# Reading a strip transpose's source over 128 partitions and planning all moves anew, in a fused attention and Mish kernel on one core

## The chip, the cores and the metric

The kernel runs on one core of a Trainium2 chip. The time is the device time of a whole execution in microseconds; lower is better. The median of three runs of the kernel before is 477.22 us (476.9 to 479.27).

## The reference, cut to what matters

One block of a transformer with modulation by a condition, all in float32. S = 2048 rows, D = 512 columns, 32 heads of 16, F = 1792 hidden columns.

```python
mod = (silu(c) @ w_mod).reshape(1, 6, 1, -1)
sa, ca, ga, sb, cb, gb = (mod[:, i] for i in range(6))
h = layernorm(x) * (1 + ca) + sa
q, k, v = heads(h @ wqkv)                      # phi(t) = where(t > 0, t + 1, exp(t)) + 1e-6
kv, z = einsum("bhsd,bhse->bhde", phi(k), v), einsum("bhsd->bhd", phi(k))
o = einsum("bhqd,bhde->bhqe", phi(q), kv) / (einsum("bhqd,bhd->bhq", phi(q), z)[..., None] + 1e-6)
x = x + ga * (o @ wo)
h = layernorm(x) * (1 + cb) + sb
x = x + gb * (mish(h @ w1 + b1) @ w2)          # mish(t) = t * tanh(softplus(t))
```

## The kernel before, in words

The 2048 rows are four row blocks (b = 0 to 3) of 512 rows, each of four strips of 128 rows (t = 0 to 3). A product of float32 accuracy is three matmuls of rounded parts: every operand is split into an upper part (name ending in h, made by ACT, L1034) and a rest (ending in l, made by VectorE, L1040), and h·h, h·l and l·h are added up.

The first part of the program, to about 190 us, is the attention. After it comes the second layer norm of every strip (`norm_job`): sums, a small rsqrt chain rs_n partly on POOL (L348), the normalization (on ACT for b < 2, else on ACT or VectorE in turn, L359), and a store of the normalized strip to the DRAM buffer nd (L389). The FFN's first product needs the normalized block with columns on the partitions. `squares_job` therefore reads nd back in an order in which VectorE's transposes of 32x32 squares (L1530, y_n to hf_n) finish the full transpose; the reads are L1521, four per row block, and each waits for all four stores of its row block. ACT scales and shifts the four chunks hf_n (L1533). Meanwhile the strips of x + ga·o themselves (the tiles r) are completed by accumulating loads r<-in_x_dram on POOL ("joins", L1578) and stored to the output (L838), which the end of the program reads again.

The FFN works on two halves, row blocks 0 and 1 (L = 0) and 2 and 3 (L = 2), and both products are done by a scheme with seven multiplications in place of eight: `pair` multiplies for pair g of 0 to 6 (256 hidden columns) into p_a, p_s and others (L1259), with operands a and s from w1 (pieces w1p, read as two DMAs per pair in `rows_job`, L1058, sums s at L1079) and b and t from hf_n; ACT copies a partial result to u (L1274), VectorE adds c_a (L1280), ACT takes Mish to u_a (L1283), which is split into l_m for `unit`'s seven products m1 to m7 with w2 (pa to pd, L1344; their weights wt_m are DMAs from w2d and w2t).

Nothing of this order is written by hand. `drive` fixes the order in which every engine's instructions are issued, with a planner: every piece of work is a job with a due time and an earliest time, `best_job` takes for each engine the due job that can start, and `emit` moves a model clock on. DMAs may go to either queue, SP or POOL (ANY), whichever is free by the model. A load's model cost is one number, `late`:

```python
wire[0] = max(wire[0], t0 + cost + 1.4) + late
late = wire[0] + 1.3 - end
```

The due times are in the table `T`; `SHIFT` moves the due time and earliest time of single jobs by name. On the chip each engine then executes its rows strictly in this order, and each DMA queue issues in its order, so a row that waits holds those behind it.

Of the kernel before, what the change touches and what calls it, by code (L numbers as in the profile page):

```python
# [27 lines left out]
TINY = 1e-6  # L28

T = {'pre': 2,  # L30
 'pre_due': 89.2,
 'pre_at': -0.2,
 'pre_step': 12.0,
 'join_at': 90.0,
 'join_due': 106.4,
 't0_due': 5.3,
 'kept': 0,
 'early': 4,
 'slack': 3.1,
# [1 line left out]
 'store_later': 8.7,  # L41
 'row_lead': 20.6,
 'columns': 90.8,
 'column_lead': 23.7,
 'rows_early': 11.9,
 'lead_a': 4,
 'lead_l': 12,
 'lead_r': 14,
 'sum_lead': 5,
 'row_0': 31.4,  # L50
 'row_step': 12.5,
 'blocks': 14.2,
 'blocks_early': 22.0,
 'out_due': 53.4,
 'out_at': 21.3,
 'early_due': 67.9,
 'early_at': -0.5,
 'norm_due': 52.1,
# [22 lines left out]
 'r_due': 2.2,
 'out01': 58.5,
 'sum_store': 9.8,
 'half_due': 8.3,
 'sums_late': 1.5,
# [28 lines left out]
 'mish': 66.7,
 'first_at': 45.4,
 'first_due': 158.9,
 'parts_first': [-1.8, 1.4, 1.9, 4.2, 7.0, 11.0, 12.4],
 'parts_last': [-1.2, 1.4, 2.8, 4.2, 6.6, 15.7, 13.0],
 'ahead_first': 2.8,
 'ahead_last': 4.3,  # L120
 'turn_right': -0.2,
 'guard': 99.0,
 'hold': -0.1,
 'near': 3.4}

SHIFT = {'blocks_job w2r 2 0': (-0.4, -1.2),
 'blocks_job w2r 3 0': (0.0, -2.6),
 'blocks_job w2r 5 0': (4.4, 12.9),
 'load_r ANY': (12.6, 0.0),
 'norm_job x1 1 0': (-3.0, 0.0),  # L130
 'norm_job x1 1 2': (2.0, 0.0),
 'norm_job x1 2 1': (-18.3, -14.8),
 'right_job r 2 m4 5': (-4.4, 0.0),
 'right_job r 2 m6 3': (4.4, 7.5),
 'rows_job w1p 0 0 0': (-1.3, 1.0),
 'rows_job w1p 0 2 0': (-2.9, 0.0),
 'rows_job w1p 0 5 0': (-1.4, 0.0),
 'rows_job w1p 0 6 0': (5.3, -9.0),
 'split_steps ACT #44': (-23.4, 0.0),
 'split_steps ACT #8': (-6.0, 0.0),  # L140
 'step cq 0 1': (7.3, 0.0),
 'step pc 2 6': (5.3, 0.0),
 'step qr 2 2 #2': (3.3, 0.0),
 'step qr 2 3': (3.2, 0.0),
 'step qr 3 0': (3.0, 0.0),
 'step x1 0 2 #2': (16.6, -12.8),
 'steps DVE': (-16.3, 0.0),
 'stores t0 0': (27.3, 0.0),
 'sums_job w2r 1 0': (-6.7, 0.0),
 'turns DVE': (0.7, 0.0)}  # L150

@with_exitstack
def block_kernel(ctx: ExitStack, tc: tile.TileContext, x, wqkv, wo, w1, b1t, w2, c, wmodt, out):
# [229 lines left out]
    nd, yd = {}, {}  # L383
# [456 lines left out]
    hf, op_b = {}, {}  # L840
# [6 lines left out]
    PE, DVE, ACT, POOL, SP, ANY = range(6)  # L847
# [20 lines left out]
    def dma_(fn, makes=(), needs=(), queue=ANY, size=LATE):  # L868
        return step_(queue, 0.0, fn, needs, makes, size)
# [5 lines left out]
    def add_job(gen, due, at=0.0):  # L875
# [639 lines left out]
    def squares_job(b):  # L1515

        for c in range(4):
            def go(q, c=c):
                if c == 0:
                    yd["n", b] = big.tile([P, 4 * 512], F32, tag="Y", name=f"y_n_{b}", bufs=YS)  # L1520
                q.dma_start(yd["n", b][32 * c:32 * (c + 1), :].rearrange("q (m s) -> q m s", s=P),  # L1521
                            nd["n", b][c, :, :].rearrange(LANES[b], q=32))
            yield dma_(go, [("y", b)] if c == 3 else (), [("n", b, t) for t in range(4)], size=1.3 * LATE,
                       queue=(ANY, SP, POOL)[T['y_queue']] if b < 2 else ANY)
# [578 lines left out]
```

## Time and profile before

| | before |
|---|---|
| median of 3 runs | 477.22 us (476.9 to 479.27) |
| profiled execution, its own time | 478.1 us |
| its span on the core | 476.4 us |
| PE busy | 465.3 us (98%) |
| DVE (VectorE) busy | 414.9 us (87%) |
| ACT busy | 333.9 us (70%) |
| HBM traffic over the span | 222 GB/s |
| granted TensorE clock | 1.00 |

Rows of the profile give a start and a duration in us, engine, line, operation, tiles, and in brackets how long the engine stood idle just before and what ended that. "POOL" and "SPq" rows of a DMA are its issue; a DMA lands later. TensorE (PE) executes in order, so what counts is where it stands still.

### The profile page before, as it was taken

The page shows a single profiled execution, that of the slowest core. Times are in us where ns is not written, and L with a number is a line of the kernel's source. Part 1 is how long each engine was busy: PE and PEld are TensorE (multiplying, and loading weights), DVE is VectorE, ACT ScalarE, POOL GpSimd, SP SyncE. Part 2 cuts the span into 40 slices and gives each one's busy share as a digit, 9 for nine tenths or more (in the row PEclk, how much of TensorE's full clock was granted, in tenths as well). Part 3 has the DMA queues.
Part 4 walks back from the last instruction along what each step waited for, and adds up shares of the span by engine and source line. Part 5 has one row for each costly group of instructions (what it writes and reads, how often), then busy time and mean ns, then how long its engine had stood idle before and what let it go on. Part 6 is the DMA issues. An engine that isn't in the chain of part 4 may idle for free.

```text
span 476.4 us, 7262 instructions
## 1 busy us (share of the span) xinstructions
PE 465.3 (98%) x2260; PEld 381.5 (80%) x2260; DVE 414.9 (87%) x808; ACT 333.9 (70%) x614; POOL 164.7 (35%) x237
## 2 busy tenths in 40 slices
PE   8999999999999999899999999999999999999996
PEld 6788888888788888677787888888888888888886
DVE  6989989888999984698998999997796596999984
ACT  6776776849758995888987998675568555555430
POOL 4684331122220442644542222412221226426340
PEclk9999999999999999999999999999999999999999
DMA  8998699257765589998599736895531569999977
GB/s 304 400 349 228 163 194 278 74 163 225 254 154 180 161 281 275 239 268 301 171 269 345 238 118 207 165 300 154 174 113 46 154 205 225 264 292 229 191 120 134
DMA packets 83800, 102.48 MB, mean 215 GB/s; under 512 B 29481, under 2 KB 55345, under 8 KB 83506
## 3 DMA queue, kind: packets, MB, share of 16 engines
q1 hardware_dynamic: 56560, 58.48, 39.3%
q0 software_dynamic: 23888, 42.49, 37.8%
q10 hardware_dynamic: 3314, 1.05, 1.1%
q8 instruction: 18, 0.29, 0.3%
q14 instruction: 20, 0.16, 0.1%
HBM read 71.57 MB, written 34.34 MB: 222 GB/s over the span
## 4 chain that ended last, share of the span: by engine, by line
PE 76%; DMA 10%; ACT 6%; DVE 4%; issue 2%; POOL 1%; ACTq 0%; SPq 0%; DVEq 0%; POOLq 0%
PE p_a L1259 13%; PE pa L1344 11%; PE pc L1344 6%; PE p_s L1259 5%; PE pd L1344 4%; DMA out_dram<-r 4%; DMA r<-in_x_dram 3%; PE pq_a L545 3%; PE pb L1344 3%; PE gacc L212 2%; PE pk L213 2%; PE pk L212 2%; PE gacc L214 2%; PE gacc L213 2%; PE pk L214 2%
## 5 line engine op out<-in xcount | busy, mean ns | idle before, releaser
L1283 ACT ACTIVATE u_a<-c_a,b1c 128x512 f32<-128x512 f32 x42 | 30.3, 720 | 18.6 <-DVE c_a L1280 16.6
L1218 POOL DMA_DIRECT2D wt_m<-w2t x27 | 22.7, 1056 | 43.5 <-ACT l_m_3h L1034 8.8
L1409 POOL DMA_DIRECT2D out_dram<-turned x20 | 24.3, 1687 | 34.3 <-DVE turned L1397 34.3
L1274 ACT ACTIVATE u<-p_a 128x512 f32<-128x512 f32 x42 | 24.8, 591 | 15.6 <-PE p_a L1259 15.2
L1280 DVE TENSOR_TENSOR c_a<-p_s,u 128x512 f32<-128x512 f32 x28 | 19.2, 686 | 6.5 <-ACT u L1274 4.2
L1218 POOL DMA_DIRECT2D wt_m<-w2d x16 | 15.1, 1143 | 14.2 <-PE pa L1344 10.2
L1233 DVE TENSOR_TENSOR u_a<-u_a,u_a 128x512 f32<-128x512 f32 x28 | 18.5, 685 | 0.0
L348 POOL TENSOR_TENSOR rs_n<-rs_n,half 128x1 f32<-128x1 f32 x16 | 11.0, 691 | 20.6 <-DVE rs_n L1487 11.6
L1058 POOL DMA_DIRECT2D w1p<-w1d x16 | 12.4, 780 | 16.2 <-DVE a_1l L1040 6.6
L1530 DVE STREAM_TRANSPOSE hf_n<-y_n 128x512 f32<-128x512 f32 x16 | 10.4, 687 | 7.4 <-DMA y_n<-nd 7.4
L443 ACT ACTIVATE e_k<-pk 128x512 f32<-128x512 f32 x15 | 8.9, 591 | 10.2 <-PE pk L214 10.2
L1533 ACT ACTIVATE hf_n<-hf_n,mc 128x512 f32<-128x512 f32 x16 | 12.1, 805 | 3.9 <-DVE hf_n L1530 3.9
L348 POOL TENSOR_TENSOR rs_x<-rs_x,half 128x1 f32<-128x1 f32 (+1 forms) x10 | 7.8, 786 | 15.9 <-DVE rs_x L343 14.7
L446 DVE SCALAR_TENSOR_TENSOR ku<-e_k,relu_k 128x512 f32<-128x512 f32 x15 | 10.7, 715 | 2.9 <-ACT relu_k L444 2.7
L1280 DVE TENSOR_TENSOR c_a<-p_a,u 128x512 f32<-128x512 f32 x14 | 9.6, 689 | 4.0 <-PE p_a L1259 3.4
L1673 DVE SCALAR_TENSOR_TENSOR q<-e_q,relu_q 128x512 f32<-128x512 f32 x16 | 10.9, 689 | 0.6 <-ACT relu_q L1669 0.6
L1040 DVE TENSOR_TENSOR l_m_4l<-u_a,l_m_4h 128x512 fp32r<-128x512 f32 x12 | 8.2, 687 | 3.4 <-ACT l_m_4h L1034 3.4
L324 DVE SCALAR_TENSOR_TENSOR wm<-wm,sc_row 128x512 f32<-128x512 f32 x16 | 10.6, 681 | 0.0
L1795 DVE SCALAR_TENSOR_TENSOR q<-q,rd 128x512 f32<-128x512 f32 x16 | 10.6, 688 | 0.0
L1311 ACT ACTIVATE u_a<-p_a,b1c 128x512 f32<-128x512 f32 x14 | 9.5, 680 | 1.5 <-PE p_a L1259 1.0
L1521 POOL DMA_DIRECT2D y_n<-nd x12 | 6.8, 575 | 10.3 <-DMA out_dram<-r 9.4
L1375 ACT ACTIVATE U<-pa,mc 128x512 f32<-128x512 f32 x10 | 6.8, 681 | 4.8 <-PE pa L1344 4.7
(1257 smaller groups left out, 1877.9 us busy)
## 6 DMA issues: line engine op xcount, KB each, us to landing
wt_m<-w2t POOLq DMA_DIRECT2D x27, 256.0 KB, 4.6
wt_m<-w2t SPq DMA_DIRECT2D x26, 256.0 KB, 5.2
w1p<-w1d POOLq DMA_DIRECT2D x16, 256.0 KB, 5.2
wt_m<-w2d POOLq DMA_DIRECT2D x16, 256.0 KB, 4.8
x<-in_x_dram SPq DMA_DIRECT2D x15, 256.0 KB, 5.1
r<-in_x_dram POOLq DMA_DIRECT2D x15, 256.0 KB, 6.3
w1d<-in_w_dram SPq DMA_DIRECT2D x4, 896.0 KB, 8.2
wm<-in_wmodt_dram SPq DMA_DIRECT2D x12, 256.0 KB, 5.3
```

Source lines behind the costliest of these rows:

```text
L212: pe.matmul(o, st[0], mv[0], start=start, stop=False)
L213: pe.matmul(o, st[0], mv[1], start=False, stop=False)
L214: pe.matmul(o, st[1], mv[0], start=False, stop=stop)
L348: pool.tensor_tensor(y, y, half[:, lo:hi], op=ALU.pow)
L1218: q.dma_start(f32(v), (w2d if src == "w2d" else w2t)[g][:, :, part, :])
L1233: dve.tensor_tensor(get(d), u, v, op=o)
L1259: pe.matmul(p, st, mv, start=onto is None and c == 0 and i == 0, stop=c == 1 and i == 2, skip_group_check=onto is not None)
L1274: act.activation(t["u", n], t["pa"], AF.Copy)
L1280: dve.tensor_tensor(t[key], t[p], t["u", n], op=ALU.add)
L1283: act.activation(u, t[key], AF.Mish, bias=b1c[:, f:f + 1])
L1344: pe.matmul(o, st[:, cs], mv, start=not onto and n == 0 and k == 0, stop=n == G - 1 and k == 2, skip_group_check=onto)
L1409: q.dma_start(rows_, sq, accum_op=ALU.add)
```

## The change

Three things are changed.

1. In `squares_job`, for row blocks 0 and 1, each of the four reads now covers all 128 partitions and 512 of the 2048 columns (2 KB per partition) where it covered 32 partitions and all columns (8 KB per partition). The four together read the same data to the same places, and the transposes need all four as before. Row blocks 2 and 3 are read as before.
2. In the table `T` 52 of the 95 values are new, `late` among them: the time that each transfer adds to the model's wire. `n_queue` goes from 0 (any queue) to 1 (SP), for the stores nd of row blocks 0 and 1; `gate_g` from 5 to 6 moves the transposition of the gate gb by one pair.
3. `SHIFT` has other entries: 25 before, 32 after, with 16 names in both.

```diff
- 'late': 0.6611,
+ 'late': 0.6637,
...
- 'n_queue': 0,
+ 'n_queue': 1,
...
- 'gate_g': 5,
+ 'gate_g': 6,
...
@@ squares_job
             def go(q, c=c):
                 if c == 0:
                     yd["n", b] = big.tile([P, 4 * 512], F32, tag="Y", name=f"y_n_{b}", bufs=YS)
+                if b < 2:
+                    part = slice(512 * c, 512 * (c + 1))
+                    q.dma_start(yd["n", b][:, part], nd["n", b][:, :, :].rearrange("c (q m) s -> (c q) (m s)", q=32)[:, part])
+                    return
                 q.dma_start(yd["n", b][32 * c:32 * (c + 1), :].rearrange("q (m s) -> q m s", s=P),
                             nd["n", b][c, :, :].rearrange(LANES[b], q=32))
```

What this does to the order of instructions is seen by comparing the two programs' rows. PE's order is the same to pair 5 of the first half (some 264 us into the execution), and then differs in the place of the gate's transpose and in the interleaving of single pair steps and units. VectorE and ACT have the same instructions in another order in many places; five DMAs more are on SP and five fewer on POOL. In the rows below the lines of the kernel after are 7 higher (11 behind `squares_job`); the last number of a name is a serial number.

**Reads of y_n.** On POOL, from the rsqrt steps of row block 1 to the reads of row block 1; y_n_2317 and y_n_2316 belong to row block 0, y_n_2420 to row block 1, n_2_2195 is strip 2 of row block 0. Before:

```order
L389 DMA nd_2112<-n_2_2195 128x4x128
L838 DMA out_dram<-r_2_1388 128x512
L348 TENSOR_TENSOR rs_n_2181<-rs_n_2181,half 128x1 x2
L1521 DMA y_n_2317<-nd_2112 32x2048
L348 TENSOR_TENSOR rs_n_2181<-rs_n_2181,half 128x1
L1521 DMA y_n_2317<-nd_2112 32x2048 x2
L838 DMA out_dram<-r_3_1404 128x512
L838 DMA out_dram<-r_1_1548 128x512
L1521 DMA y_n_2420<-nd_2249 32x2048 x4
```

And after:

```order
L355 TENSOR_TENSOR rs_n_2181<-rs_n_2181,half 128x1 x3
L1530 DMA y_n_2316<-nd_2112 128x512
L355 TENSOR_TENSOR rs_n_2181<-rs_n_2181,half 128x1
L1530 DMA y_n_2316<-nd_2112 128x512 x2
L845 DMA out_dram<-r_1_1372 128x512
L845 DMA out_dram<-r_0_1523 128x512
L845 DMA out_dram<-r_3_1592 128x512
L1530 DMA y_n_2420<-nd_2248 128x512 x4
```

The store of n_2 and the output store r_2_1388 have gone from POOL to SP, three other output stores stand between the two groups of reads, and the fourth read of row block 0 is on SP in both.

**The output stores and the first pieces of w1 for pair 2.** On SP, from the last store of row block 1 on; w1p_2_0 and w1p_2_1 are the two pieces, and the stores of r_0_2319 and behind it (r_0_2318 after) belong to row blocks 2 and 3. Before:

```order
L389 DMA nd_2249<-n_3_2355 128x4x128
L838 DMA out_dram<-r_1_1372 128x512
L838 DMA out_dram<-r_0_1525 128x512
L838 DMA out_dram<-r_2_1554 128x512
L838 DMA out_dram<-r_3_1597 128x512
L838 DMA out_dram<-r_0_2319 128x512
L838 DMA out_dram<-r_1_2359 128x512
L838 DMA out_dram<-r_1_2455 128x512
L1058 DMA w1p_2_1_2623<-w1d 128x4x128
```

After:

```order
L396 DMA nd_2248<-n_3_2354 128x4x128
L845 DMA out_dram<-r_2_1388 128x512
L845 DMA out_dram<-r_3_1404 128x512
L845 DMA out_dram<-r_1_1529 128x512
L845 DMA out_dram<-r_2_1549 128x512
L845 DMA out_dram<-r_0_2318 128x512
L845 DMA out_dram<-r_2_2378 128x512
L1065 DMA w1p_2_0_2609<-w1d 128x4x128
L845 DMA out_dram<-r_1_2359 128x512
```

The other piece is on POOL, behind the joins and output stores there. Before:

```order
L1578 DMA r_0_2444<-in_x_dram 128x512
L1578 DMA r_1_2455<-in_x_dram 128x512
L838 DMA out_dram<-r_2_2379 128x512
L838 DMA out_dram<-r_3_2398 128x512
L838 DMA out_dram<-r_0_2444 128x512
L1058 DMA w1p_2_0_2609<-w1d 128x4x128
```

After:

```order
L1589 DMA r_0_2444<-in_x_dram 128x512
L1589 DMA r_1_2455<-in_x_dram 128x512
L1589 DMA r_1_2359<-in_x_dram 128x512
L845 DMA out_dram<-r_3_2398 128x512
L845 DMA out_dram<-r_0_2444 128x512
L845 DMA out_dram<-r_1_2455 128x512
L1065 DMA w1p_2_1_2615<-w1d 128x4x128
```

The pieces have changed queues: SP's now stands behind two stores of these row blocks where it stood behind three, POOL's behind the store of r_1_2455 (strip 1 of row block 3). Strip 1 of row block 2, r_1_2359, is joined last of six where it was second.

**The normalization of r_3_3 and the pieces of w1 for pair 5.** On VectorE, strip 3 of row block 3, r_3_2579 before and r_3_2575 after. Before:

```order
L324 SCALAR_TENSOR_TENSOR wm_2654,mc<-wm_2654,sc_row 128x512
L1040 TENSOR_TENSOR l_m_3l<-u_a_3_3016,l_m_3h 128x512
L1079 TENSOR_TENSOR s_4_3049<-w1p_4_1_2955 128x256
L1040 TENSOR_TENSOR t_2l<-t_2_2868,t_2h 128x512
L1079 TENSOR_TENSOR s_4_3049<-s_4_3049,w1p_4_0_2940 128x256
L1040 TENSOR_TENSOR a_4l<-w1p_4_0_2940,a_4h 128x512
L1079 TENSOR_TENSOR s_4_3050<-w1p_4_0_2940,w1p_4_1_2955 128x256
L359 TENSOR_SCALAR r_3_2579<-r_3_2579,mv_n_2815,rs_n_2751 128x512
```

After:

```order
L1047 TENSOR_TENSOR t_2l<-t_2_2869,t_2h 128x512
L366 TENSOR_SCALAR r_3_2575<-r_3_2575,mv_n_2811,rs_n_2751 128x512
L1047 TENSOR_TENSOR l_m_3l<-u_a_3_3016,l_m_3h 128x512
L1047 TENSOR_TENSOR t_2l<-t_2_2868,t_2h 128x512
L1086 TENSOR_TENSOR s_4_3052<-w1p_4_1_2955 128x256
```

On POOL the store of this strip (nd_2918<-r_3) and the pieces of w1 behind it. Before:

```order
L1521 DMA y_n_2973<-nd_2718 32x16x128 x2
L1164 DMA w2d_2992<-b_3_0_2938 128x512
L348 TENSOR_TENSOR rs_n_2751<-rs_n_2751,half 128x1
L389 DMA nd_2918<-r_3_2579 128x4x128
L1058 DMA w1p_5_0_3096<-w1d 128x4x128
L1058 DMA w1p_5_1_3114<-w1d 128x4x128
```

After:

```order
L396 DMA nd_2918<-r_2_2570 128x4x128
L1139 DMA w2r_1_2996<-in_w_dram 128x512
L355 TENSOR_TENSOR rs_n_2751<-rs_n_2751,half 128x1
L1532 DMA y_n_2992<-nd_2717 32x16x128
L396 DMA nd_2918<-r_3_2575 128x4x128
L1065 DMA w1p_5_0_3093<-w1d 128x4x128
L1065 DMA w1p_5_1_3111<-w1d 128x4x128
```

The normalization comes seven rows earlier on VectorE; on POOL the same store and pieces follow each other, behind another store and a load of w2 that were on SP.

More of the change, by code (lines that the diff above doesn't have):

```diff
@@ L30 @@
 T = {'pre': 2,
- 'pre_due': 89.2,
- 'pre_at': -0.2,
- 'pre_step': 12.0,
+ 'pre_due': 98.7,
+ 'pre_at': -0.8,
+ 'pre_step': 12.1,
  'join_at': 90.0,
- 'join_due': 106.4,
- 't0_due': 5.3,
+ 'join_due': 113.2,
+ 't0_due': 4.8,
  'kept': 0,
@@ L43 @@
  'columns': 90.8,
- 'column_lead': 23.7,
+ 'column_lead': 22.4,
  'rows_early': 11.9,
  'lead_a': 4,
- 'lead_l': 12,
- 'lead_r': 14,
+ 'lead_l': 13,
+ 'lead_r': 15,
  'sum_lead': 5,
@@ L52 @@
  'blocks': 14.2,
[L53 to L58, printed above, removed]
+ 'blocks_early': 22.8,
+ 'out_due': 57.9,
+ 'out_at': 22.8,
+ 'early_due': 67.7,
+ 'early_at': 0.8,
+ 'norm_due': 52.8,
  'norm_at': 15.7,
  'norm_step': 3.8,
- 'squares_due': 81.8,
+ 'squares_due': 78.4,
  'turn_due': 79.9,
- 'turn_step': 2.0,
+ 'turn_step': 2.1,
  'mm': 0.2277,
  'slow': 1.0194,
- 'late': 0.6611,
+ 'late': 0.6637,
  'pool_issue': 1.1494,
- 'left_early': 17.6,
+ 'left_early': 13.7,
  'right_due': 1.2,
@@ L74 @@
  'pace_l': 3.4,
- 'pair_l': 15.6,
+ 'pair_l': 16.1,
  'seq_0': 'ABCD.E.FG',
  'seq_l': 'AB.CD.E.F.G.',
- 'copy_due': 10.0,
- 'result_due': 1.4,
+ 'copy_due': 10.3,
+ 'result_due': 1.5,
  'soon': 9.4,
[L81 to L85, printed above, removed]
+ 'r_due': 1.5,
+ 'out01': 56.9,
+ 'sum_store': 8.0,
+ 'half_due': 8.1,
+ 'sums_late': 0.4,
  'first': 0,
- 'turn_late': [8.3, 2.8],
- 'left_out': 10.0,
+ 'turn_late': [8.3, 3.2],
+ 'left_out': 10.5,
  'add': 4.2,
@@ L90 @@
  'behind': 3.5,
- 'den01': 26.7,
- 'den23': 33.3,
+ 'den01': 26.6,
+ 'den23': 26.5,
  'm_at': 33.9,
  'out': [43.3, 56.3, 59.3, 78.4],
- 'res_early': 36.5,
- 'mod_at': 17.9,
- 'gate_g': 5,
+ 'res_early': 36.3,
+ 'mod_at': 18.5,
+ 'gate_g': 6,
  'rd_size': 0.9,
  'rd_wait': 2.6,
- 'x1_due': 99.5,
- 'x1_at': [85.0, 86.9, 85.0, 90.0],
- 'rd_at': [2.5, -1.7, -0.5, 0.0],
+ 'x1_due': 98.2,
+ 'x1_at': [85.0, 86.9, 84.2, 97.3],
+ 'rd_at': [-4.0, -1.7, -1.4, 0.0],
  'rd_queue': 0,
- 'n_queue': 0,
+ 'n_queue': 1,
@@ L105 @@
  'y_queue': 0,
  'row_at': 1.8,
- 'turn0': 66.8,
- 'turn1': 66.3,
- 'norm0': [43.2, 66.8],
+ 'turn0': 67.3,
+ 'turn1': 66.0,
+ 'norm0': [44.3, 66.8],
  'ffn': 66.8,
  'rows01_early': 55,
- 'gate_due': 166.7,
+ 'gate_due': 168.6,
  'gate_at': 113.2,
[L114 to L129, printed above, removed]
+ 'mish': 66.2,
+ 'first_at': 44.3,
+ 'first_due': 150.6,
+ 'parts_first': [-1.8, 3.1, 1.9, 4.2, 7.0, 10.7, 14.2],
+ 'parts_last': [-1.2, 1.4, 3.2, 4.2, 6.6, 15.7, 13.0],
+ 'ahead_first': 2.6,
+ 'ahead_last': 4.4,
+ 'turn_right': -0.8,
+ 'guard': 94.7,
+ 'hold': -0.7,
+ 'near': 2.8}
+SHIFT = {'blocks_job w2r 2 0': (4.3, -1.2),
+ 'blocks_job w2r 5 0': (1.7, 13.6),
+ 'left_job s3 0 1 #2': (0.0, 6.4),
@@ L130 @@
  'norm_job x1 1 0': (-3.0, 0.0),
  'norm_job x1 1 2': (2.0, 0.0),
[L132 to L137, printed above, removed]
- 'rows_job w1p 0 6 0': (5.3, -9.0),
- 'split_steps ACT #44': (-23.4, 0.0),
- 'split_steps ACT #8': (-6.0, 0.0),
- 'step cq 0 1': (7.3, 0.0),
+ 'norm_job x1 2 1': (-28.8, -1.7),
+ 'norm_job x1 2 2': (6.5, 0.0),
+ 'norm_job x1 3 2': (0.0, -6.2),
@@ L142 @@
+ 'phi_job exp 1 0': (-2.6, 0.0),
+ 'phi_job exp 1 2': (0.2, 0.0),
+ 'right_job r 0 m5 3': (0.0, 7.2),
+ 'right_job r 2 m1 5': (7.0, -10.6),
+ 'rows_job w1p 0 2 0': (-0.9, 0.0),
+ 'rows_job w1p 0 5 0': (-2.1, 0.0),
+ 'rows_job w1p 0 6 0': (5.3, -9.0),
+ 'rows_job w1p 2 2 0': (0.0, 4.2),
+ 'rows_job w1p 2 3 0': (0.0, 0.4),
+ 'split_steps ACT #19': (-3.0, 0.0),
+ 'split_steps ACT #8': (-6.6, 0.0),
+ 'split_steps hf 1 3': (25.3, 0.0),
+ 'step cq 0 1': (9.6, 0.0),
  'step pc 2 6': (5.3, 0.0),
@@ L145 @@
  'step qr 3 0': (3.0, 0.0),
[L146 to L150, printed above, removed]
+ 'step rd 0 3': (-0.8, 0.0),
+ 'step t 0 t2 1': (-1.3, 0.0),
+ 'step t 0 t4 0': (5.8, 0.0),
+ 'step x1 2 1': (-8.3, 5.3),
+ 'stores t0 0': (32.1, 0.0),
+ 'sums_job w2r 1 0': (-3.8, 0.0),
+ 'sums_job w2r 3 0': (3.1, 2.5)}
 @with_exitstack
```

## The prediction

> **What bounds the kernel now.** I read the page first, then PE's busy time by stages, then the list of who waited for whom, and last the instructions around each wait in order of time.
>
> On the page, PE is busy 98% of the span; the two DMA queues share the transfers, and one issue group gives the median time to landing of w1p loads:
>
> ```profile
> span 476.4 us, 7262 instructions
> PE 465.3 (98%) x2260; PEld 381.5 (80%) x2260; DVE 414.9 (87%) x808; ACT 333.9 (70%) x614; POOL 164.7 (35%) x237
> ...
> q1 hardware_dynamic: 56560, 58.48, 39.3%
> ...
> w1p<-w1d POOLq DMA_DIRECT2D x16, 256.0 KB, 5.2
> ```
>
> By stages (stretch in us, length, then busy us), all PE time to be had behind the first stage lies before 270 us:
>
> ```profile
> 190.00:270.00 80.00, 75.36 (x321) 1.00 0.92 264
> ...
> 270.00:470.00 200.00, 200.00 (x915) 1.00 0.75 184
> ```
>
> So 4.64 us are lost between 190 and 270 and none after it; what is won there arrives at the end whole, if the second half stays gapless. PE's waits between 190 and 270 (total, times, longest) name them, 4.5 us in all:
>
> ```profile
> PE p_a L1259 <- ACT b_0h L1034: 2.1, 1, 2.1
> PE pa L1344 <- DVE l_m_0l L1040: 1.0, 1, 1.0
> PE p_s L1259 <- DVE c_a L1280: 0.9, 2, 0.6
> PE p_a L1259 <- ACT u L1274: 0.3, 1, 0.3
> PE p_a L1259 <- DVE b_0l L1040: 0.2, 1, 0.2
> ```
>
> The first wait, in order of time (start, us, engine): the four loads of y_n for row block 0 are issued, the first on POOL at 178.40, the last on SP at 181.74; VectorE stands still 5.91 us for the last landing; then come four transposes, four scalings on ACT, the split b_0h, and PE:
>
> ```profile
> 178.40 0.55 POOL L1521 DMA_DIRECT2D y_n<-nd  x1
> ...
> 181.74 0.39 SPq L1521 DMA_DIRECT2D y_n<-nd  x1
> ...
> 189.64 2.49 DVE L1530 STREAM_TRANSPOSE hf_n<-y_n 128x512 f32<-128x512 f32 x4 [5.91 <-DMA y_n<-nd]
> ...
> 193.22 0.61 ACT L1034 ACTIVATE b_0h<-hf_n 128x512 fp32r<-128x512 f32 x1
> ...
> 191.13 0.39 PE L213 MATMUL o<-m_3l,qs_3h 128*128 128x512 f32 x1
> 191.35 0.39 PE L214 MATMUL o<-m_3h,qs_3l 128*128 128x512 f32 x1
> 193.89 0.50 PE L1259 MATMUL p_a<-b_0h,a_0h 128*128 128x512 f32 x1 [2.14 <-ACT b_0h L1034]
> ```
>
> Matmuls in a row start 0.22 to 0.23 us apart (the first two PE rows), so this stall cost 193.89 − 191.35 − 0.23 = 2.31 us, 0.17 more than its wait says.
>
> The second: the last store of row block 1's normalized rows is issued on SP at 183.58, behind the SP load of y_n; POOL sits 9.40 us before it can issue row block 1's four loads, and VectorE gets them at 199.68. From there it is busy without a pause, and the split l_m_0l, which PE wants, comes at 210.49:
>
> ```profile
> 183.58 1.05 SPq L389 DMA_DIRECT2D nd<-n  x1
> ...
> 192.14 1.97 POOL L1521 DMA_DIRECT2D y_n<-nd  x4 [9.40 <-DMA out_dram<-r]
> ...
> 199.68 0.71 DVE L1530 STREAM_TRANSPOSE hf_n<-y_n 128x512 f32<-128x512 f32 x1 [1.45 <-DMA y_n<-nd]
> ...
> 210.49 0.68 DVE L1040 TENSOR_TENSOR l_m_0l<-u_a,l_m_0h 128x512 fp32r<-128x512 f32 x1
> ```
>
> The third and fourth are smaller: VectorE waits 1.69 and 1.53 us for w1p pieces. The first of them was issued on SP at 208.80, behind a store; the second on POOL behind the store nd<-r, for which POOL waited 5.72 us on the DVE normalization of 245.87:
>
> ```profile
> 208.80 0.38 SPq L1058 DMA_DIRECT2D w1p<-w1d  x1
> ...
> 218.44 0.43 DVE L1079 TENSOR_TENSOR s<-w1p 128x256 f32<-128x256 f32 x1 [1.69 <-DMA w1p<-w1d]
> ...
> 243.06 0.69 DVE L1040 TENSOR_TENSOR l_m_3l<-u_a,l_m_3h 128x512 fp32r<-128x512 f32 x1
> ...
> 245.87 0.54 DVE L359 TENSOR_SCALAR r<-r,mv_n,rs_n 128x512 f32<-128x512 f32 x1
> 246.71 0.80 POOL L389 DMA_DIRECT2D nd<-r  x1 [5.72 <-DVE r L359]
> 247.50 2.98 POOL L1058 DMA_DIRECT2D w1p<-w1d  x4
> ...
> 256.65 0.42 DVE L1079 TENSOR_TENSOR s<-w1p 128x256 f32<-128x256 f32 x1 [1.53 <-DMA w1p<-w1d]
> ```
>
> **The change, part by part.**
>
> *The shape of the eight loads.* Bytes and count stay, and the issue took about 0.5 us for either shape: 1.97 us for the four above, 1.07 for two plain loads of 128 partitions.
>
> ```profile
> 292.20 1.07 POOL L1176 DMA_DIRECT2D w2q<-in_w_dram  x2 [2.42 <-PE pa L1344]
> ```
>
> What changes is the time on the DMA engines. The software queue's packets, megabytes and share of 16 engines: first 192.5 to 199.5, mostly 32-partition reads; then 292.2 to 296, plain 128-partition loads of 2 KB rows; then 200 to 206, accumulating 128-partition loads.
>
> ```profile
> q0 software_dynamic: 320, 1.30, 90.2%
> ...
> q0 software_dynamic: 160, 0.52, 47.2%
> ...
> q0 software_dynamic: 588, 1.07, 98.1%
> ```
>
> One megabyte costs 0.902 x 7.0 / 1.30 = 4.86 us of all 16 engines in the first, 0.472 x 3.8 / 0.52 = 3.45 in the second, 0.981 x 6.0 / 1.07 = 5.50 in the third, and 0.393 x 476.4 / 58.48 = 3.20 on the hardware queue over the span. For the 1.05 MB of a row block the change is then worth 1.5 us by the second; the ends are a gain of 1.7 (hardware queue) and a loss of 0.7 (accumulating). I take 1.5: same queue, shape and kind as the new loads.
>
> The Trainium skill (SBUF — State Buffer, section "Door 1: The DMA port swizzle") says that a transfer to partitions 0 to 31 reaches 8 of 16 ports, at most 218 GB/s, and one to all 128 reaches 436. By that rule a row block would gain 2.4 us (estimate from that page), and the sum below would be some 1 us larger; the 1.30 MB in 90.2% of 7 us, 206 GB/s, agree with the lower rate, while the second row's 290 GB/s stays well short of the upper.
>
> *First stall.* Last landing 1.5 us earlier, so VectorE, ACT and PE too: the waits for b_0h and b_0l, 2.3 us in all, become 0.8. **−1.5.** The cover of a further gain is PE's own work until 191.35.
>
> *Second stall.* The store of 183.58 shares the engines with these reads and lands as much earlier, 1.5; the reads behind it add their own 1.5. VectorE begins 3.0 us earlier against a PE that is 1.5 earlier, so the 1.0 goes. **−1.0.** Late next is VectorE's string of work from there.
>
> *Planned moves between 170 and 220.*
>
> ```profile
> 171.04 7.30 SPq L389 DMA_DIRECT2D nd<-n  x3
> ```
>
> All eight stores of normalized rows are now on SP (one had been on POOL); SP took the others from 171.04 on and stood waiting between them for most of 7.30 us, so one more costs nothing. The output store that stood on POOL ahead of row block 0's loads is now on SP, behind the store of 183.58. The first w1p piece for pair 2 stands on SP ahead of one output store, and the second on POOL behind the output store of r_3_1, the fifth join instead of the sixth. Both queues run about 3 us earlier through the reads, and PE wants them about 2.5 earlier; with the store that is passed, that just covers the third wait of 0.65 (0.6 in the list, the longest of the c_a row). **−0.6.** The ends are 0 and −0.65.
>
> *Planned moves between 240 and 260.* VectorE's normalization of r_3_3 is seven rows earlier, just ahead of the l_m_3l of 243.06, where it stood at 245.87. POOL's nd<-r and the four w1p loads behind it follow by 2.8 us, more than the 1.53 that VectorE waited. The two PE waits here, 0.3 and 0.9 − 0.65, go. **−0.5.** Passed on POOL: one more nd store (0.80 by the row above) and a w2r load (about 0.5, as above), in time in which POOL stood waiting.
>
> *All else* (the gate's transpose from pair 5 to pair 6, the phi order, w1p moved from SP to POOL at 111, the order of many ACT and DVE rows): nothing, since PE waited for nothing from 270 on and the moved loads had long landed. The nearest case to the edge: VectorE now reads the second w1p piece of pair 0 at about 125, ahead of q; it is issued on POOL right behind the first,
>
> ```profile
> 110.30 0.77 POOL L1058 DMA_DIRECT2D w1p<-w1d  x1 [3.47 <-PE pq_a L545]
> ```
>
> so it lands near 110.30 + 0.77 + 5.2 = 116.3 by the page's median. If the cover of the rest is gone, each us that VectorE is late from 264 on is a us of PE.
>
> **Sum.** −1.5 − 1.0 − 0.6 − 0.5 = −3.6; the stalls' 0.17 beyond the wait, at the three that go, make it −4.1; small new waits in orders shifted everywhere, 0.1: −4.0. Against the profiled execution: span 476.4 − 4.0 = 472.4, plus the 1.7 around it (its own time is 478.1) 474.1. That execution stood 0.9 above the median of the runs, so 473.2 for the median.
>
> **Rivals.**
>
> *Landing is not transfer.* Least, median and most time to landing of row block 1's four reads, and of the five w2q loads:
>
> ```profile
> DMA to landing us min/median/max: 3.6/4.8/5.8
> ...
> DMA to landing us min/median/max: 2.8/2.9/3.2
> ```
>
> If a read's time is mostly a fixed part, only 3.6 − 2.8 = 0.8 us per row block is won: −0.8 at the first stall, 0 at the second (both sides 0.8 earlier), −1.1 by the planner: 477.2 − 1.9 = 475.3, no change. The Trainium skill (DMA: Bandwidth & Descriptors, section "Anatomy of one DMA — SWDGE (gpsimd) path") speaks for it: some 2 us of a transfer are completion latency, whatever its shape. Against it: 4.8 and 5.8 at the third and fourth show a queue that drains, not a constant. Chance 0.11.
>
> *The gain is given back in the next stage.* From 264 to 288 ACT and VectorE have nothing to spare (PE, PEld, DVE, ACT, POOL):
>
> ```profile
> 264.00:288.00 24.00, 24.00 (x107) 19.80 (x107) 23.70 (x43) 23.98 (x45) 7.51 (x12) 1.00 0.57 185
> ...
> DVE c_a L1280 <- ACT u L1274: 4.2, 5, 1.6
> ```
>
> A PE that comes 4 us earlier meets an ACT that must have made up the same 4 us before 264. If ACT has made up only half, 2.0 come back: 475.2, no change. For it: the saturation. Against: both engines start earlier by the same landings, and ahead of it both had time over, ACT 4.5 and VectorE 1.8 of 24 us:
>
> ```profile
> 240.00:264.00 24.00, 23.46 (x103) 18.71 (x102) 22.17 (x49) 19.48 (x36) 6.96 (x10) 1.00 1.06 309
> ```
>
> Chance 0.10.
>
> *Slower.* The same place: the u, c_a, u_a ring between ACT and VectorE in the pair steps from 264 on, whose rows are reordered in nearly every step (the gate's row and a scaling of row block 3 are new there). The longest wait in that ring was 1.6 us. Four such, at four pair steps, cost 6.4, which turns −4.0 into +2.4: 479.6. It decides from 4.0 us of new PE waits on. For it: the multiset of work is unchanged and there is no slack on ACT. Against: every wait of that ring left PE untouched before. Chance 0.13.
>
> **How the numbers follow.** Forecast 0.66; the two middling rivals 0.21; slower 0.13. 0.5% of 477.2 is 2.4 us, about what a measurement of this kernel can tell from no change: faster below 474.8, slower above 479.6. The low end: all 4.64 us of 190 to 270 gone, with 0.17 at six waits, −5.7, and up to 1.2 more in waits that no row lists: 470.3. The high end takes in the middling rivals and the near half of the slower case: 478.3. The forecast's own range is 470.3 to 474.7.
>
> **What would show it.** Right: the software queue under 4 us of 16 engines per megabyte while y_n is read; VectorE's wait before the first transpose shorter by 1.5; PE's wait for b_0h under 1.0; no PE wait for l_m_0l; VectorE's waits for w1p gone; PE 200.00 of 200.00 in the second half. Wrong: a first transpose still near 189; PE waits for u, c_a or wt_m behind 264; new waits between 110 and 160.

## The result, and the profile after

The kernel after takes 473.9 us (median of 5 runs, 473.49 to 474.49) beside 477.22 of the kernel before: a ratio of 0.993, 95% interval 0.9908 to 0.9952, faster by 0.7%. The forecast was 473.2. The profiled execution took 473.9, 1.7 of it around the span. On the page of the kernel after:

```profile
span 472.2 us, 7260 instructions
...
PE 464.1 (98%) x2260; PEld 382.5 (81%) x2260; DVE 414.7 (88%) x808; ACT 332.1 (70%) x614; POOL 163.0 (35%) x232
```

PE by stages (stretch, length, then busy us and instructions of each engine). PE has ended at 467.9 here, so the second stretch stops before that:

```profile
190.00:270.00 80.00, 77.82 (x338) 62.65 (x338) 74.30 (x157) 73.35 (x138) 35.12 (x49) 1.00 0.92 270
...
270.00:466.00 196.00, 196.00 (x899) 163.51 (x898) 171.82 (x300) 117.02 (x208) 63.35 (x82) 1.00 0.74 185
```

The loss between 190 and 270 went from 4.64 to 2.18 us, and PE got through 338 matmuls in it where there were 321; from 270 on it still has no gap. Its waits in that stretch, from the list of who waited for whom:

```profile
PE p_a L1266 <- ACT b_0h L1041: 1.4, 1, 1.4
...
PE pa L1351 <- DVE l_m_0l L1047: 0.4, 1, 0.4
PE p_a L1266 <- DVE b_0l L1047: 0.2, 1, 0.2
```

The waits for c_a and u, those behind the third and fourth stall, are gone; the first two are smaller. At the first stall, in order of time (start, us, engine), the last read of row block 0, VectorE's transposes behind it, and PE:

```profile
181.39 0.39 SPq L1530 DMA_DIRECT2D y_n<-nd  x1
...
188.47 2.49 DVE L1541 STREAM_TRANSPOSE hf_n<-y_n 128x512 f32<-128x512 f32 x4 [5.13 <-DMA y_n<-nd]
...
192.72 0.50 PE L1266 MATMUL p_a<-b_0h,a_0h 128*128 128x512 f32 x1 [1.37 <-ACT b_0h L1041]
```

At the second, the last store of row block 1, its four reads, the first transpose, and the split that PE wants:

```profile
183.04 0.83 SPq L396 DMA_DIRECT2D nd<-n  x1
...
192.25 2.13 POOL L1530 DMA_DIRECT2D y_n<-nd  x4 [9.33 <-DMA out_dram<-r]
...
198.54 2.49 DVE L1541 STREAM_TRANSPOSE hf_n<-y_n 128x512 f32<-128x512 f32 x4 [1.50 <-DMA y_n<-nd]
...
208.75 0.68 DVE L1047 TENSOR_TENSOR l_m_0l<-u_a,l_m_0h 128x512 fp32r<-128x512 f32 x1
```

The reads are issued no earlier than before (192.14), but VectorE has them 1.14 earlier. At the third and fourth stall VectorE finds its w1p pieces there, with no bracket behind its rows:

```profile
207.06 0.78 POOL L1065 DMA_DIRECT2D w1p<-w1d  x1
...
215.62 0.42 DVE L1086 TENSOR_TENSOR s<-w1p 128x256 f32<-128x256 f32 x1
...
239.99 0.78 POOL L396 DMA_DIRECT2D nd<-r  x1 [1.48 <-DVE r L366]
240.76 2.23 POOL L1065 DMA_DIRECT2D w1p<-w1d  x3
...
251.74 0.38 DVE L1086 TENSOR_TENSOR s<-w1p 128x256 f32<-128x256 f32 x1
```

One reading orders the traces below. Take the start of row block 1's transposes on VectorE (198.54 above; 199.68 before), which I call the landing, and PE's last matmul. Where that row has no bracket, as in two traces below, the data was there before VectorE was. Here are the last matmuls, of the kernel before and then of the kernel after:

```profile
471.95 0.28 PE L214 MATMUL m<-wt_m,l_m_5l 128*128 128x256 f32 x1
```

```profile
467.58 0.28 PE L221 MATMUL m<-wt_m,l_m_5l 128*128 128x256 f32 x1
```

Before, the distance is 471.95 − 199.68 = 272.27; after, 467.58 − 198.54 = 269.04. I call it the tail. So of the 4.37 us between these two executions, 3.23 lie in the tail and 1.14 in the landing. The experiments ask which part of the change made which, and what the landing hangs on. Against the medians, 0.9 of the 4.37 is the execution of before that was profiled, which stood that much above its median.

### The profile page after: what moved, and what is told of

Its sections match the earlier page's. It is cut to its first block, busy times and chain, and to the rows that moved or that the text cites. A ratio compares the mean times of both kernels' runs of the same rounds, so it can differ in the third digit from the quotient of the medians.

```text
span 472.2 us, 7260 instructions
## 1 busy us (share of the span) xinstructions
PE 464.1 (98%) x2260; PEld 382.5 (81%) x2260; DVE 414.7 (88%) x808; ACT 332.1 (70%) x614; POOL 163.0 (35%) x232
## 3 DMA queue, kind: packets, MB, share of 16 engines
q10 hardware_dynamic: 3314, 1.05, 1.1%
## 4 chain that ended last, share of the span: by engine, by line
PE 81%; DVE 9%; ACT 5%; DMA 2%; issue 1%; POOL 1%; SPq 0%; ACTq 0%; DVEq 0%
PE p_a L1266 18%; PE pa L1351 12%; PE p_s L1266 7%; PE pc L1351 6%; PE pb L1351 4%; PE pd L1351 4%; PE pq_a L552 3%; PE gacc L219 2%; PE gacc L221 2%; PE pk L221 2%; PE pk L219 2%; PE gacc L220 2%; PE pk L220 2%; DMA out_dram<-r 1%; PE pq L219 1%; PE pq L221 1%
## 5 line engine op out<-in xcount | busy, mean ns | idle before, releaser
L1225 POOL DMA_DIRECT2D wt_m<-w2t x29 | 24.0, 1153 | 48.9 <-ACT u_a L1290 11.1
L1416 POOL DMA_DIRECT2D out_dram<-turned x20 | 22.5, 1702 | 35.7 <-DVE turned L1404 24.1
L1065 POOL DMA_DIRECT2D w1p<-w1d x18 | 13.7, 760 | 25.0 <-PE p_s L1266 8.2
L355 POOL TENSOR_TENSOR rs_n<-rs_n,half 128x1 f32<-128x1 f32 x16 | 12.5, 790 | 17.7 <-DVE rs_n L1494 12.5
L1225 POOL DMA_DIRECT2D wt_m<-w2d x13 | 11.7, 1001 | 11.3 <-DVE c_a L1287 3.9
L1041 ACT ACTIVATE l_m_6h<-u_a 128x512 fp32r<-128x512 f32 x12 | 7.3, 621 | 5.1 <-DVE u_a L1240 5.1
L1047 DVE TENSOR_TENSOR l_m_6l<-u_a,l_m_6h 128x512 fp32r<-128x512 f32 x12 | 8.2, 684 | 2.6 <-ACT l_m_6h L1041 2.6
```

The lines of the kernel that those rows point to most:

```text
L355: pool.tensor_tensor(y, y, half[:, lo:hi], op=ALU.pow)
L1225: q.dma_start(f32(v), (w2d if src == "w2d" else w2t)[g][:, :, part, :])
L1416: q.dma_start(rows_, sq, accum_op=ALU.add)
```

## Experiments

The kernels ran in four groups, each beside runs of the kernel before, whose medians were 477.8, 477.9, 477.4 and 477.52 us. Ratios are to these, with 95% intervals.

**1. The new reads alone, and the new tables alone** (kernel before with the four added lines of `squares_job`; kernel after without them).

```diff
  shape_only, to the kernel before:
+                if b < 2:
+                    part = slice(512 * c, 512 * (c + 1))
+                    q.dma_start(yd["n", b][:, part], nd["n", b][:, :, :].rearrange("c (q m) s -> (c q) (m s)", q=32)[:, part])
+                    return
  tables_only, to the kernel after: the same four lines with -
```

> The kernel before with only the shape of the eight reads changed; the planner counts both shapes alike, so every queue and engine keeps its old order. Theory A (the reads' time on the DMA engines sets the first two stalls, as predicted): y_n of row block 0 lands 1.5 us earlier, row block 1's 3.0, PE's wait for b_0h falls from 2.1 to under 0.9, l_m_0l's wait goes; median 474.4 to 474.8. Theory B (read off the two traces: the last read is held by the other transfers in the queues, the shape is worth 0.8): b_0h's wait about 1.4, l_m_0l's 0.4 to 0.8, the waits at 227 and 260 stay; median 475.5 to 476.3. Theory C (the planner did it all): within 0.5 of 477.2.

> The kernel after with the eight reads in their old shape, all tables and so all orders as after. Theory A: the two small stalls at 227 and 260 go (1.1 to 1.4), the first two stay at 2.1 and 1.0; median 475.8 to 476.1. Theory B: the planned orders are worth more than half, the stalls at 227 and 260 are worth 1.7 by starts of matmuls in a row, and 0.4 more elsewhere: 474.9 to 475.5. A rival: the orders fit only the faster reads, and something late is uncovered: 477 or more.

Measured: the reads alone 475.79 us, ratio 0.9971 (0.9949 to 0.9993); the tables alone 475.66, 0.9951 (0.9931 to 0.9970). The two gains, 0.29% and 0.49%, add up to 0.78%, about the 0.70% of both. Row block 1's transposes and PE's end, in the trace with the reads alone and then with the tables alone, the second with its largest wait of PE:

```profile
198.08 2.48 DVE L1534 STREAM_TRANSPOSE hf_n<-y_n 128x512 f32<-128x512 f32 x4
...
468.80 0.28 PE L214 MATMUL m<-wt_m,l_m_5l 128*128 128x256 f32 x1
```

```profile
PE p_s L1266 <- DVE t_0l L1047: 1.4, 1, 1.4
...
199.55 2.49 DVE L1537 STREAM_TRANSPOSE hf_n<-y_n 128x512 f32<-128x512 f32 x4 [3.00 <-DMA y_n<-nd]
...
468.63 0.28 PE L221 MATMUL m<-wt_m,l_m_5l 128*128 128x256 f32 x1
```

With the tables alone the landing is where it was (199.55 against 199.68), and the tail is 269.08, that of the kernel after to 0.04. So the tables alone give the whole shorter tail. PE's wait for b_0h is only 0.3 here; what that saved comes back as 1.4 for t_0l, the split of row block 1's data. The time lies between those expected under theories A and B.

With the reads alone the transposes start 1.60 earlier, and the tail is 270.72, 1.55 shorter than before with no row moved: the wait at 227 is gone, that at 260 is there (0.3 for c_a). The time is that of theory B, the waits are not. Two rows explain more. VectorE does not wait for row block 1 here: its transposes stand behind c_a, for which it waited on PE's first product of row block 0. And the w1p piece of the third stall is issued on SP no earlier than before (208.99 against 208.80), but VectorE could use it at once at 215.49, at most 6.5 us later, where it took 9.64 before (218.44):

```profile
197.47 0.69 DVE L1280 TENSOR_TENSOR c_a<-p_a,u 128x512 f32<-128x512 f32 x1 [1.15 <-PE p_a L1259]
...
215.49 0.42 DVE L1079 TENSOR_TENSOR s<-w1p 128x256 f32<-128x256 f32 x1
```

Whether the reads' shape or the chance of one execution brought the piece sooner, one profile does not tell.

**2. The kernel after once more**, unchanged, to see how far one profile can be trusted.

> The kernel after once more, beside the next one on the same chip, and for a second profile of the reads. If the landing of the last read of row block 0 varies from one execution to the next by as much as the shape was to give (5.8 to 7.4 us over three programs with the same rows up to there), it will lie in that band again and not at 7.0; the time at 473.5 to 474.5.

Measured: 474.48 us, ratio 0.9933 (0.9908 to 0.9958), so the result stands. Its trace:

```profile
PE p_a L1266 <- ACT b_0h L1041: 2.1, 1, 2.1
PE p_s L1266 <- DVE t_0l L1047: 0.9, 1, 0.9
...
200.41 2.49 DVE L1541 STREAM_TRANSPOSE hf_n<-y_n 128x512 f32<-128x512 f32 x4 [2.36 <-DMA y_n<-nd]
...
469.44 0.28 PE L221 MATMUL m<-wt_m,l_m_5l 128*128 128x256 f32 x1
```

The same program, and the first stall is as long as before the change (2.1), while the landing is 1.87 later than in the first profile and 0.73 later than in the kernel before. The tail is 269.03. What the two profiles of one kernel share is the tail; what differs is the landing. This execution, of 475.76 us, was the slowest of its seven. The shorter first stall of the first profile can therefore not be put down to the new reads.

**3. ACT's scalings spread among the splits.** The first stall has a second handle: ACT scales all four chunks before it splits the first. Here a chunk's scaling is issued just before the split that needs it, and all else stays in place.

```diff
+            if name == "b21_0_0":
+                run_scales(2)
...
-            act.activation(hf[b, j], hf[b, j], AF.Identity, bias=mc[:, 12 + j:13 + j], scale=mc[:, 16 + j:17 + j])
+            go = lambda: act.activation(hf[b, j], hf[b, j], AF.Identity, bias=mc[:, 12 + j:13 + j],
+                                        scale=mc[:, 16 + j:17 + j])
+            if b == 0 and j:
+                scales.append((j, go))
```

> The kernel after with every row of every engine where it was, except that ACT splits chunk 0 of row block 0 right behind its own scaling, and so on for the four chunks, in place of four scalings and then four splits. PE can begin row block 0 about 1.9 us earlier against the landing of y_n. If VectorE's chain behind y_n of row block 1 is the next bound: the wait for b_0h goes and as much appears at t_0l or l_m_0l, 473.4 to 474.4. Rival, the first stall counts in full: 472.3 to 472.9.

Measured: 473.84 us, ratio 0.9921 (0.9908 to 0.9935), no different from the kernel after.

```profile
PE p_s L1272 <- DVE t_0l L1053: 0.8, 1, 0.8
PE p_a L1272 <- DVE b_0l L1053: 0.6, 2, 0.3
PE p_a L1272 <- DVE b_1l L1053: 0.4, 2, 0.2
...
199.84 2.49 DVE L1553 STREAM_TRANSPOSE hf_n<-y_n 128x512 f32<-128x512 f32 x4 [2.34 <-DMA y_n<-nd]
...
468.90 0.28 PE L221 MATMUL m<-wt_m,l_m_5l 128*128 128x256 f32 x1
```

The wait for b_0h is not in the list any more, small ones and t_0l stand in its place, and the tail is 269.06. With the wait for b_0h at 1.4, 0.3, 2.1 and none, the tail was 269.04, 269.08, 269.03 and 269.06. While VectorE waits for row block 1 (here 2.34), the first stall adds nothing to the end: PE that starts row block 0 earlier only waits for row block 1. The two chains are not independent, though. Ahead of the transposes VectorE makes c_a of row block 0, so where row block 1 is there in time, as in `shape_only`, PE's start on row block 0 sets theirs.

**4. The store ahead of the reads.** If row block 1's landing sets the end, what sets the landing? Its reads wait for the store nd of strip 3. (POOL's row names an output store as what ended its wait, but nd lands at 183.04 + 8.6 = 191.6, 0.6 before the reads go out.) In `hold_by_hand` (to the kernel after) the two w2t stores from t_0 and the output stores of row blocks 0 and 1 that stand ahead of this store on SP are issued behind it, and those ahead of the reads on POOL behind the reads. `hold_old_shape` is the same with the old reads, `hold_scale` the same with experiment 3, `hold_before` the same in the kernel before.

```diff
+    def later(key, fn):
+        if key in gone:
+            fn()
+        else:
+            held[key].append(fn)
...
-        queue.dma_start(x1d[b][P * t:P * (t + 1), :], xt["r", b, t])
+        r = xt["r", b, t]
+        go = lambda: queue.dma_start(x1d[b][P * t:P * (t + 1), :], r)
+        if b < 2:
+            later("sp" if queue is sp else "pool", go)
...
+                to_dram("n", b, t, st[1], q)
+                if (b, t) == (1, 3):
+                    let_go("sp")
...
  hold_old_shape, to hold_by_hand:
-                if b < 2:
+                if False:
```

> The kernel after with every row where it was, except that on SP the two t0 stores and one output store stand behind the last store nd of row block 1 and on POOL three output stores stand behind row block 1's four reads. If the transfers ahead in the queues hold that store (theory B): it lands at about 187.5 in place of 191.7, POOL issues row block 1's reads at 188 in place of 192.3, y_n of row block 1 is there at 193 to 194.5 (198.4), that of row block 0 at 186.5 to 187.5, and of the 3 us that PE still loses between 190 and 215 about 2 go: 471.5 to 472.5. If landing is a fixed part: within 0.5 of 473.9.

> hold_by_hand with the eight reads in the old shape, 32 partitions each: the price of the shape where little else is in the queues. Theory A (1.5 us of the DMA engines per row block): the four reads of row block 1 take about 7.3 us from the first issue to the last landing against 5.6 to 6 in hold_by_hand, and PE waits again for what hangs on row block 1: 0.5 to 1.5 us above hold_by_hand. If the shape is worth nothing by itself: no difference in the span of the reads nor in time.

> Both edits of scale_by_hand and hold_by_hand. If the two stalls stand one behind the other, the second bounding what the first can give, both together give more than the sum of each: PE loses under 1 us between 190 and 215, 470.7 to 471.7. Rival: VectorE has no time over from 200 on and gives back what is won: 472 or more.

> The kernel before, old tables and old reads, with only the order of stores changed as in hold_old_shape: t0 and one output store behind the last store nd of row block 1 on SP, three output stores behind row block 1's reads on POOL. If the queue ahead of that store set the first two stalls, both go without the change's help (3.3 of the 7 us that PE lost) and the stalls at 227 and 260 stay or shrink: 473 to 475 beside 477.5. If those two stalls need the new tables: 476 or more. If late w1p pieces follow the same queue: the stall at 227 goes too, 472.5.

Measured: 471.92 us, ratio 0.9893 (0.9875 to 0.9911); 472.05, 0.9884 (0.9870 to 0.9897); 472.12, 0.9885 (0.9872 to 0.9899); 476.43, 0.9978 (0.9956 to 1.0). The store by its issue group (out<-in, engine, count, KB, median us to landing), of the kernel after and of `hold_old_shape`; then the latter's reads and end:

```profile
nd<-n SPq DMA_DIRECT2D x1, 256.0 KB, 8.6
```

```profile
nd<-n SPq DMA_DIRECT2D x1, 256.0 KB, 3.8
...
187.31 1.93 POOL L1562 DMA_DIRECT2D y_n<-nd  x4 [6.14 <-DMA nd<-n]
...
196.24 2.49 DVE L1573 STREAM_TRANSPOSE hf_n<-y_n 128x512 f32<-128x512 f32 x4 [1.43 <-DMA y_n<-nd]
...
465.77 0.28 PE L221 MATMUL m<-wt_m,l_m_5l 128*128 128x256 f32 x1
```

Issued within 0.1 us of where it was (182.97 against 183.04), the store lands 4.9 earlier, the reads go out 4.9 earlier and land 2.3 earlier: the slowest of them takes 7.4 us to landing, where it took 4.6 in the kernel after and 5.9 in `tables_only`. The tail is 269.53. This is the version that beats both kernels: 472.0 in three forms, some 1.8 us under 473.84, the median of experiment 3's kernel in the same group, which did as well as the kernel after. Old and new reads differ by 0.13 us here. The third form was expected at 470.7 to 471.7 and gains nothing on top, though in the trace of `hold_by_hand` VectorE starts at 197.27 straight behind c_a, with no wait for row block 1.

In the kernel before the same hold brings the landing to 196.49, 3.2 earlier, yet the time only falls by 0.2% (476.43 where 473 to 475 was expected). VectorE's wait for the w1p piece at the third stall and PE behind it:

```profile
216.05 0.42 DVE L1098 TENSOR_TENSOR s<-w1p 128x256 f32<-128x256 f32 x1 [2.50 <-DMA w1p<-w1d]
...
217.92 0.50 PE L1282 MATMUL p_a<-b_0h,a_2l 128*128 128x512 f32 x1 [0.81 <-DVE a_2l L1059]
...
469.11 0.28 PE L214 MATMUL m<-wt_m,l_m_5l 128*128 128x256 f32 x1
```

The wait there grew from 1.69 to 2.50, and the tail is 272.62: the piece is issued only 0.9 earlier than before (207.90), behind the same store on SP, and part of the gain became a longer wait. Single runs reach from 473.42 to 478.02; what the slower of them look like no profile shows.

**5. One row of SP's order.** In the kernel before, the piece w1p that makes VectorE wait at 218.44 is put ahead of the store of strip (3, 1) on SP, once alone and once with the hold. Nothing else moves.

```diff
+    waiting = []
...
+        if (b, t) == (3, 1):
+            waiting.append(go)
...
+            if (l, g, i) == (0, 2, 1):
+                for go in waiting:
+                    go()
```

> The kernel before with one row moved: on SP the second w1p piece of pair 2 stands ahead of the output store of r_3_1, for which SP waited until 208. If its place behind that store sets the third stall: the piece is issued at about 202, lands by 210, VectorE's wait of 1.7 for it and PE's 0.65 at 227 go, nothing else moves: 0.7 less, 476.3 to 477 beside 477.2. Rival, the time after issue counts (the joins hold the engines): it lands after 214 and the stall stays.

> hold_before with that same row moved. hold_before won 3 us at the first two stalls and lost 0.81 and 0.66 again where VectorE stood 2.50 for the same piece. If the piece is what took the gain: both PE waits at 218 and 225 go and the time falls to 474 to 475.2 (hold_before 476.4 with a wide spread); the wait at 259 stays. Rival, VectorE itself is behind by then: the waits move to another producer, 476.

Measured: 476.31 us, ratio 0.9972 (0.9959 to 0.9984), and with the hold 473.43, 0.9913 (0.9895 to 0.9931). With the hold:

```profile
201.02 0.57 SPq L1080 DMA_DIRECT2D w1p<-w1d  x1
...
213.62 0.42 DVE L1104 TENSOR_TENSOR s<-w1p 128x256 f32<-128x256 f32 x1
...
467.09 0.28 PE L214 MATMUL m<-wt_m,l_m_5l 128*128 128x256 f32 x1
```

The piece is issued at 201.02 where it was 207.90 in `hold_before`, the waits of 2.50 and 0.81 are gone, and with the landing at 196.63 the tail is 270.46; alone it is 270.64. The one row is worth 1.6 to 2.2 us of tail (272.27 to 270.64, and 272.62 to 270.46), 1.2 on the median alone and 3.0 between the two held kernels, more than was expected there (474 to 475.2). `shape_only`, in which that wait was gone without the row, has a like tail of 270.72. What remains to 269.04, 1.4 to 1.7, is left for the rest of the tables, the fourth stall among them; no run takes it apart.

**6. The same two ideas by way of the planner.** An earlier due time for the first split, and the hold as a dependence of the output and w2t stores.

```diff
  split_first, to the kernel after:
- 'parts_first': [-1.8, 3.1, 1.9, 4.2, 7.0, 10.7, 14.2],
+ 'parts_first': [-4.2, 3.1, 1.9, 4.2, 7.0, 10.7, 14.2],
  hold, to the kernel after:
-            add_job(iter([dma_(lambda q: x1_store(b, t, q), (), [("x1", b, t)])]), T['x1_due'], T['x1_at'][b])
+            add_job(iter([dma_(lambda q: x1_store(b, t, q), (), [("x1", b, t)] + ([("n", 1, 3)] if b < 2 else []))]),
+                    T['x1_due'], T['x1_at'][b])
```

> The kernel after with one due time moved, so that ACT makes the first split b_0h behind two scalings instead of four. PE can then start row block 0's first product about 1.4 us earlier and its first wait (1.4 us) goes. Theory B1 (VectorE's chain behind y_n of row block 1 is the next bound): the wait for l_m_0l at 209 grows from 0.4 to about 1.5 and the time stays within 0.5 of 473.9. Rival: the first stall is worth its full length at the end: 472.5.

> The kernel after with the eight output stores of row blocks 0 and 1 and the two w2t stores t0 of group 0 planned behind the last store of row block 1's normalized rows, so the two DMA queues hold little else while y_n is read. If the other transfers in the queues hold the reads (theory B): y_n of row block 0 lands at 185 to 186.5 (188.4 after), the last store of row block 1 at about 186.5 (191.7), POOL issues row block 1's reads at 187 (192.3), both PE waits go, 2 us less up to there; what the later stores cost is open, 472 to 473.5 in all. If landing is mostly a fixed part: y_n lands within 0.7 us of 188.4, no gain.

Measured: 479.79 us, ratio 1.0045 (1.0024 to 1.0066), and 489.88, 1.0251 (1.0219 to 1.0283). In both the planner then put rows elsewhere in another order, and the tails are 273.8 and 285.2. The longest wait in the second, on VectorE and then on PE:

```profile
219.59 0.55 DVE L366 TENSOR_SCALAR r<-r,mv_n,rs_n 128x512 f32<-128x512 f32 x1 [5.48 <-DMA out_dram<-r]
...
221.73 0.79 PE L1351 MATMUL pb<-l_m_0l,b 128*128 128x512 f32 x1 [5.60 <-DVE l_m_0l L1047]
```

The normalization writes r in place, so it waits for the output store of r, which the planner now sent late, and l_m_0l stands behind it. Both miss what was expected (472.5 to 474.4, and 472 to 473.5) and, with other rows moved, do not test the idea; by hand the same hold gains 1.8. Here a table of due times fitted under one set of rules did not suit another.

## Why the prediction was right, and where it was not

The number came out (473.2 against 473.9), the direction too, but from another sum. The prediction gave the reads 2.5 of the gain and the tables 1.1 (1.4 with the part beyond the waits). The runs give the tables 3.2 in the tail and 0.49% or 2.3 us of the time (2.1 between the medians), and the reads between nothing (with the hold) and 0.29% or 1.4 us (alone; 2.0 between the medians). That the total came within 0.7 us is in part luck: the reads were priced too high by about as much as the tables were too low. Of the signs that it named for being right, the shorter wait before the first transpose (5.13 and 5.84 for 5.91, not 1.5 less), a wait for b_0h under 1.0 (1.4 and 2.1) and none for l_m_0l (0.4 and 0.5) did not come; its sign for being wrong, a first transpose still near 189, did (188.47 and 189.48). The signs for the w1p waits and the second half came.

*The shape of the reads, 1.5 per row block: mis-sized.* The software queue while y_n is read, in the kernel after, in the same 7 us as before:

```profile
q0 software_dynamic: 494, 1.38, 78.9%
```

0.789 x 7.0 / 1.38 = 4.00 us of 16 engines per megabyte, where it was 4.86 and the prediction said under 4 and used 3.45. For 1.05 MB that is 0.9, not 1.5. In the same stretch the five traces with new reads and no hold by hand (`after`, `after_again`, `shape_only`, `scale_by_hand`, `split_first`) give 3.99 to 4.22, the three with old ones (`before`, `tables_only`, `w1p_before`) 4.65 to 5.35.

It hardly shows in the landing: row block 1's transposes began at 199.68, 199.55 and 199.31 with the old reads (before, `tables_only`, `w1p_before`), and at 198.08, 198.54, 199.84 and 200.41 with the new (`shape_only`, after, `scale_by_hand`, `after_again`), means of 199.5 and 199.2. In 7 executions of this spread a gain of 0.3 is not told from none. But the earliest was the fastest of its kernel's twelve runs and the two latest the slowest of theirs, and the runs do show a gain: under the new tables 475.66 with the old reads against 473.9, 474.48 and 473.84 with the new (`scale_by_hand` the last), in different groups, by ratios 0.2 to 0.3%. With the hold there was none on the median (472.05 with the old, 471.92 with the new).

By the Trainium skill (SBUF — State Buffer, "Door 1: The DMA port swizzle") 32 partitions have half of the ports, and a row block would gain 2.4 us (estimate from that page, for four reads one after the other). No run here shows so much; the measurement decides. The rival "landing is not transfer" was nearer on this point, with 0.8 per row block. The least time to landing of row block 1's reads is 3.6 us in both shapes (before and `shape_only`). The Trainium skill (DMA: Bandwidth & Descriptors, "Anatomy of one DMA — SWDGE (gpsimd) path") states a fixed part of some 2 us; the 3.6 us leave room for it, but no run here separates it from the transfer. The rival's 475.3 failed on the tables, which it took at 1.1.

*First stall, −1.5: the step failed as structure.* The wait fell by 0.77 in one profile and by 0.04 in the other, and experiment 3 took it away with no gain. It was summed with the second stall as if in series; but while VectorE still waits for row block 1's data, PE passes the second no earlier because it passed the first earlier.

*Second stall, −1.0: the outcome about as said, the reason not.* The wait for l_m_0l fell from 1.0 to 0.4 and 0.5, not to none. The store that was to land 1.5 earlier landed no earlier: POOL could issue the reads at 192.25 (192.14 before). Only other stores taken from its way moved it (8.6 to 3.8 us).

*Third stall, −0.6: right in mechanism, too small.* Moving the piece ahead of one store is enough. The list of waits understates what it cost; PE's rows around the wait in the kernel before:

```profile
226.66 0.39 PE L1259 MATMUL p_a<-b_1h,a_2l 128*128 128x512 f32 x1
227.69 0.50 PE L1259 MATMUL p_s<-t_0h,s_2h 128*128 128x512 f32 x1 [0.65 <-DVE c_a L1280]
228.03 0.39 PE L1259 MATMUL p_s<-t_0l,s_2h 128*128 128x512 f32 x1
```

From 226.66 to 228.03 are 1.37 us for two matmuls that otherwise start 0.23 apart: 0.91 lost for a wait listed as 0.65, 0.26 more (the prediction took 0.17), and small gaps that no list names come on top. The tail says 1.6 to 2.2.

*Fourth stall, −0.5: right in mechanism, by this count too small.* POOL's nd<-r is at 239.99 for 246.71, the w1p pieces behind it 6.7 earlier, VectorE no longer waits. The two PE waits there are 0.27 and 0.26 in the list; with 0.26 more each they cost some 1.05, and the tail leaves 1.4 to 1.7 for this and all else. No run tests it alone.

*The rivals "given back from 264 to 288" and "slower" did not come.* PE has no gap behind 270, and there are no waits for u, c_a or wt_m in the kernel after. Waits for u behind 264 appear where a due time or a rule was changed (2.2 us in all in `split_first`, 2.6 in `hold`), so the danger was real and this plan avoids it.

Open: why the w1p piece of the third stall landed about 3 us sooner in `shape_only`, at the same place in the queue, and why the landing of row block 1 wanders over 2.3 us between executions.

## What to carry to other kernels

Where an engine waits twice in a row for data that two chains deliver, the later chain sets the end for as long as it is the later: measure from that delivery to the end, and see whether the distance or the delivery moved, before summing the waits. A store that a later read depends on should go out ahead of the stores that nothing waits for. Under the new tables that took the kernel with the old reads from 475.66 to 472.05 (in two groups), where the new reads took it to some 474; in the kernel before, with the w1p piece still late, it gave 0.2%. Do not read a change of a microsecond in one DMA's landing from one profile of each kernel: profile the same kernel twice first.

## What the runs showed of the hardware

Here the time to landing of a transfer depended on what stood ahead of it, not only on its size. The store nd of 256 KB took 7.8 to 8.6 us to landing, in five traces of the new tables, with two w2t stores, an output store and the read of y_n shortly ahead of it on its queue, and 3.8 to 4.9 with the three stores behind it. And the same SP read of row block 0, 256 KB, unheld, took from 5.6 to 7.8 us: in the kernel before and with its new tables alone, old reads in both,

```profile
y_n<-nd SPq DMA_DIRECT2D x1, 256.0 KB, 7.8
```

```profile
y_n<-nd SPq DMA_DIRECT2D x1, 256.0 KB, 5.9
```

and 7.0 and 7.7 in the two profiles of the kernel after, in which every row is the same. This spread is larger than the effect that the change of shape was predicted to have.
